# An inverse DFT stage contracted 64 partitions at a time, without the transfers that rearranged its input

## The chip, the core and the metric

One NeuronCore of a Trainium2 chip runs the whole program in one launch. The metric is the device time of one execution in microseconds (us). TensorE (PE) multiplies; its weight loads have a row of their own (PEld). VectorE (DVE) and ScalarE (ACT) work on tiles and read the accumulators; GpSimd (POOL) and SyncE (SP) here only issue DMAs.

## The reference

`x` has 4 batches of 3072 x 256. A frequency mix comes first, then two feed-forward layers. Only the mix is touched by the change.

```python
X = np.fft.rfft(x, axis=1)
Yr = Xr @ w_r - Xi @ w_i + b_r
Yi = Xr @ w_i + Xi @ w_r + b_i
Yr = np.sign(Yr) * np.maximum(np.abs(Yr) - lam, 0.0)      # lam = 0.01, Yi likewise
y = np.fft.irfft(Yr + 1j * Yi, n=3072, axis=1)
# then: k = relu(xk @ w_k); v = (k*k) @ w_v; r = sigmoid(xr @ w_r); x = r * v
# then: h = x @ w_in; out = (h * clip(h + 3, 0, 6) / 6) @ w_out
```

## The kernel before

The transform of 3072 points is split into 96 x 32. `s1` does the 96-point part of a batch `b` in eight steps and stores it to DRAM. `mid(b)` loads it back in 12 chunks `j` (`NP = 12`); each chunk has two frequency groups of 64 rows. `ib` does the last 96-point part of the inverse. What follows (`u_r`, `u_k`, `u_v`) is the first feed-forward layer, in units of 12 matmuls over 512 columns, and then the second layer.

Inside `mid(b)`, chunk `j` goes through:

- `s2(j)`: the 32-point transform, 8 PE instructions, whose output `X` is split by ACT and DVE into a high and a low part (`Xh`, `Xl`).
- `mix(j)`: 18 matmuls over 256 columns, then two kinds of DVE adds into `y` (`yf`), a ReLU on ACT into `m` (`ym`), and one DVE pass (L379) that ends the soft threshold. `y` is laid out [128 partitions, 2, 256]: the partitions hold the two groups, 64 each, and the middle index the real and the imaginary part.
- L380 to L382: four DMAs on SP move quadrants of `y` into `z` (`yz`), so that each group's real and imaginary rows together fill 128 partitions.
- `split_y(j)` (batches 1 to 3 only): ACT and DVE split `z` into `yh` and `yl`.
- `ia(j)`: the 32-point inverse. In batches 1 to 3 these are three matmuls for each of two groups (high x high, low x high, high x low; the type is a rounded 32-bit float), in batch 0 one full 32-bit matmul for each group, which is two PE instructions. All contract 128 partitions. ACT copies the accumulator to `iasb` (L403) and SP stores it.

The order is written out by hand: step `j` of `mid` does `s2(j)`, then, after a yield, `split_y(j - 2)` and `mix(j - 1)`, then, after another yield, `ia(j - behind)`; `behind` is `BEHIND[b]`, 3 for batch 0 and 2 for the others. The last DVE pass of chunk `j` and its four DMAs are issued at the beginning of step `j + 2`. The `mid` of batches 1 to 3 and `s1`, `ib` are interleaved with the feed-forward layer: between two yields of `mid` one or two units of 12 matmuls run. In batch 0 nothing else but weight decoding on ACT and DVE runs beside it. The tables `tt` (three buffers) are loaded by POOL; a tile holds the forward table of one chunk and the inverse table of the chunk `behind` it. The last `ia` of a batch are called from the next part through `ends`.

Each engine takes its instructions in program order, so an ACT instruction that waits holds all ACT instructions behind it.

Of the kernel before, what the change touches and what calls it, by code (L numbers as in the profile page):

```python
# [23 lines left out]
TOK = 512  # L24
NT = S // TOK
LAM = 0.01
BEHIND = (3, 2, 2, 2)
AHEAD = 7

CHUNKS = (1, 2, 3, 4, 5, 6, 7, 0)  # L30
# [19 lines left out]
def _tables():  # L50

    th = 2 * np.pi / S
    n1 = np.arange(N1)
    n2 = np.arange(N2)
    f1 = np.zeros((N1, N1))
    f1[:, 0] = 1.0
    f1[:, 1] = (-1.0) ** n1
    for u in range(1, 48):
        f1[:, 2 * u] = np.cos(2 * np.pi * u * n1 / N1)
        f1[:, 2 * u + 1] = -np.sin(2 * np.pi * u * n1 / N1)  # L60
    fwd = np.zeros((NG, 2, 2, N2, 4, 2, N2))
    inv = np.zeros((NG, 2, 2, N2, 2, 2, N2))
    for g in range(NG):
        for uu in range(2):
            u = 2 * g + uu
            m = np.zeros((2, N2, 2, N2))
            w = np.zeros((2, N2, 2, N2))
            if u:
                k = u + N1 * np.arange(N2)
                s = np.where(k <= S // 2, 1.0, -1.0)  # L70
                c, z = np.cos(th * np.outer(n2, k)), np.sin(th * np.outer(n2, k))
                m[0, :, 0], m[1, :, 0] = c, z
                m[0, :, 1], m[1, :, 1] = -z * s, c * s
                w[0, :, 0], w[1, :, 0] = c.T * 2 / S, (-z * s).T * 2 / S
                w[0, :, 1], w[1, :, 1] = z.T * 2 / S, (c * s).T * 2 / S
            else:
                for j in range(N2):
                    src = 0 if j < 16 else 1
                    f = N1 * j if j < 16 else N1 // 2 + N1 * (j - 16)
                    c, z = np.cos(th * f * n2), np.sin(th * f * n2)  # L80
                    if j == 0:
                        alt = (-1.0) ** n2
                        m[0, :, 0, 0], m[0, :, 1, 0] = 1.0, alt
                        w[0, 0, 0], w[1, 0, 0] = 1.0 / S, alt / S
                    else:
                        m[src, :, 0, j], m[src, :, 1, j] = c, -z
                        w[0, j, src], w[1, j, src] = c * 2 / S, -z * 2 / S
            m = np.concatenate([m, m.sum(2, keepdims=True), 0 * m[:, :, :1]], 2)
            if u == 0:
                m[0, :, 2, 0], m[0, :, 3, 0] = 1.0, alt - 1.0  # L90
                m[:, :, 0:2, 0] = 0.0
            fwd[g, uu, :, :, :, uu] = m
            inv[g, :, uu, :, uu] = w
    fwd = fwd.reshape(NP, 2, 128, 256).transpose(0, 2, 1, 3)
    inv = inv.reshape(NP, 2, 128, 128).transpose(0, 2, 1, 3)
    ext = fwd[0, :, 0, 128:256].astype(np.float32)
    tab = np.zeros((NP + BEHIND[1], 128, 2, 448), np.float32)
    tab[:NP, :, :, 0:192] = fwd[:, :, :, 0:192]
    tab[BEHIND[1] :, :, :, 192:448] = np.concatenate(_pair(inv), 3)
    tab0 = np.zeros((NP + BEHIND[0], 128, 2, 320), np.float32)  # L100
    tab0[:NP, :, :, 0:192] = fwd[:, :, :, 0:192]
    tab0[BEHIND[0] :, :, :, 192:320] = inv
    small = np.concatenate([f1, f1.T], 1).astype(np.float32)
    return [np.ascontiguousarray(a) for a in (tab, tab0, ext, small)]

# [2 lines left out]
def fourier_mix_ffn_kernel(  # L108
# [45 lines left out]
    def ptile(name):  # L154
        return ps.tile([128, 1024], F32, tag="h", name=name)
# [87 lines left out]
    with tc.manual_schedule(engines=order):  # L243
# [68 lines left out]

        def load_t(b, j):

            k = BEHIND[b]
            if j >= NP + k:
                b, j = b + 1, j - NP - k
            if b < B:
                if pad_t:
                    pad(fp, pad_t.pop())  # L320
                t = fp.tile([128, 2, 448], F32R if b else F32, tag="t", bufs=3, name="tt")
                c = slice(0 if j < NP else 192, 192 if j < BEHIND[b] else 448 if b else 320)
                eng = nc.gpsimd if b or j > 2 else nc.scalar
                eng.dma_start(out=t[:, :, c], in_=(tab if b else tab0)[j, :, :, c])
                tt[b, j] = t

        def mid(b):
            gb = sc_b[b].rearrange("(j g c) n d -> j (c n) g d", g=2, c=4)
            xx, yy = {}, {}
            behind = BEHIND[b]  # L330

            def s2(j):
                (a,) = take(1)
# [15 lines left out]
            def mix(j):  # L349
                xh, xl = xx.pop(j)  # L350
                p = ptile("mix")
                k1 = p[:, 512:768]
                part = lambda k, n=128: [
                    ((xh[:, dt, 128 * k : 128 * k + n], xl[:, dt, 128 * k : 128 * k + n]), dt) for dt in range(2)
                ]
                by = lambda w, xs: [(x, (w[0][:, dt], w[1][:, dt])) for x, dt in xs]
                three(k1, by(aw[0], part(2)))
                if pad_y:
                    pad(fp, pad_y.pop())
                y = fp.tile([128, 2, D], F32, tag="y", bufs=2, name="yf")  # L360
                m = fp.tile([128, 2, D], F32, tag="co", bufs=1, name="ym")
                z = fp.tile([128, 2, D], F32, tag="z", bufs=2, name="yz")
                if b:
                    yh = fp.tile([128, 512], F32R, tag="yh", bufs=2, name="yh")
                    yl = fp.tile([128, 512], F32R, tag="yl", bufs=2, name="yl")
                bs = bias[:, 0:2] if j else bias[:, 0::2]
                three(p[:, 0:256], by(aw[2], part(1)))
                pi = by(aw[1], part(0))
                three(p[:, 256:512], pi[:1], last=False)
                if j == 0:  # L370
                    three(p[0:64, 256:512], by(aw[0], part(3, 64)), first=False, last=False)
                three(p[:, 256:512], pi[1:], first=False)
                for a in range(2):
                    nc.vector.tensor_add(y[:, a], k1, bs[:, a])  # L374
                nc.vector.tensor_add(y, y, p[:, 0:512].rearrange("p (a e) -> p a e", a=2))  # L375
                yield
                nc.scalar.activation(m, y, AF.Relu, bias=lam2, scale=-1.0)
                yield
                nc.vector.scalar_tensor_tensor(y, m, -1.0, y, op0=ALU.mult, op1=ALU.max)  # L379
                for g in range(2):  # L380
                    for a in range(2):
                        nc.sync.dma_start(out=z[64 * a : 64 * a + 64, g], in_=y[64 * g : 64 * g + 64, a])  # L382
                z = z.rearrange("p g e -> p (g e)")
                yy[j] = (z, yh, yl) if b else z

            def split_y(j):
                if b:
# [2 lines left out]

            def ia(j):
                y = yy.pop(j)
                t = tt.pop((b, j + behind))[:, :, 192:448]
                p = ptile("ia") if b else pa.tile([128, 512], F32, tag="acc", name="ia0")
                for g in range(2):
                    c = slice(256 * g, 256 * g + 256)
                    if not b:
                        nc.tensor.matmul(p[:, c], t[:, g, 0:128], y[:, c], start=True, stop=True)
                        continue
                    yh, yl = y  # L400
                    three(p[:, c], [((t[:, g, 0:128], t[:, g, 128:256]), (yh[:, c], yl[:, c]))])
                sb = fp.tile([128, 2, D], F32, tag="ia", bufs=2, name="iasb")
                nc.scalar.activation(sb.rearrange("p g d -> p (g d)"), p[:, 0:512], AF.Copy)  # L403
                nc.sync.dma_start(out=gb[j], in_=sb)

            rest = iter(())
            for j in range(NP + 1):
# [2 lines left out]
                    s2(j)  # L410
                if b or j:
                    load_t(b, j + 2)
                if j < NP:
                    yield
                    if j >= 2:
                        split_y(j - 2)
                if j:
                    rest = mix(j - 1)
                    next(rest)
                    fetch(AHEAD if b or j > 6 else 6)  # L420
                    next(rest)
                    yield
                if behind <= j < NP:
                    ia(j - behind)
            next(rest, None)
            split_y(NP - 2)

            def end(j):
                if j == NP - 1:
                    ready.add(("b", b))  # L430
                ia(j)
                if not b and j < NP - 1:
                    load_t(b, j + 6)

            if b:
                ends.extend([lambda: end(NP - 2), lambda: (load_t(b, NP + 3), split_y(NP - 1)), lambda: end(NP - 1)])
            else:
                ends.extend([lambda: end(NP - 3), lambda: end(NP - 2), lambda: end(NP - 1)])

        ysb = {}  # L440

# [435 lines left out]
        def stream(parts):  # L877

            for kind, part in parts:
                if kind == "ib":  # L880
                    if ends:
                        while ends:
                            ends.pop(0)()
                            yield
                        for _ in range(3):
# [223 lines left out]
```

## Time and profile before

| what | value |
|---|---|
| median of three runs | 2034.64 us (2031.91 to 2035.55) |
| the profiled execution | 2030.07 us |
| its span, first to last instruction | 2028.3 us |
| PE busy | 1949.9 us, 96% of the span |
| DVE, ACT busy | 1424.9 us (70%), 1240.8 us (61%) |
| granted TensorE clock, mean | 0.976 |

The profile is of one execution. A granted clock of 1.00 is 2.4 GHz and 0.50 is 1.2 GHz. A matmul's record is longer than its turn on the engine, because matmuls overlap; the time between two starts is what one costs. A wait names the engine that waits, the line, what it waits for, the total, how often, and the longest.

### The profile page before, as it was taken

What the parts mean: (1) busy time and instruction counts of PE and PEld (TensorE: products, weight loads), DVE (VectorE), ACT (ScalarE), POOL (GpSimd) and SP (SyncE); (2) the same over time, 40 slices, a digit from 0 to 9 for tenths busy, and PEclk for the clock granted to TensorE, in tenths of its full rate; (3) what the DMA queues carried; (4) which work ended last, traced back from release to release, by engine and by line L of the source; (5) the groups of instructions that cost most, each with busy time, mean ns of one, the idle gap of its engine ahead of it and who ended that gap; (6) DMA issues with size and microseconds to landing.
All of it is one profiled execution on the core that took longest, in us unless ns stands there. A gap on an engine that the chain in (4) does not pass through costs nothing.

```text
span 2028.3 us, 32930 instructions
## 1 busy us (share of the span) xinstructions
PE 1949.9 (96%) x13352; PEld 1776.3 (88%) x13352; DVE 1424.9 (70%) x1813; ACT 1240.8 (61%) x1766; POOL 35.5 (2%) x61
## 2 busy tenths in 40 slices
PE   6889989998999999999999999999999999999998
PEld 3758777887688778888889999999999999999998
DVE  1756664565456655777768788877887788788876
ACT  2455545454544545777756677667776777677765
POOL 0100000000000000000000000000000000000000
PEclk7979999998999899999999999999999999999999
DMA  8786446544663343222110011001100011001100
GB/s 251 213 255 193 124 119 208 178 136 113 196 189 107 103 140 122 78 86 87 64 42 22 22 32 32 22 22 29 30 28 22 24 31 32 22 23 32 32 11 22
DMA packets 121161, 177.18 MB, mean 87 GB/s; under 512 B 16129, under 2 KB 78209, under 8 KB 121009
## 3 DMA queue, kind: packets, MB, share of 16 engines
q1 hardware_dynamic: 110016, 152.91, 25.0%
q0 software_dynamic: 8768, 20.95, 3.9%
q8 instruction: 105, 1.72, 0.4%
q10 hardware_dynamic: 2224, 1.22, 0.3%
q14 instruction: 48, 0.39, 0.1%
HBM read 99.13 MB, written 63.31 MB: 80 GB/s over the span
## 4 chain that ended last, share of the span: by engine, by line
PE 77%; DVE 8%; DMA 6%; ACT 4%; SPq 3%; issue 1%; ACTq 0%; DVEq 0%
PE oacc L857 25%; PE rq L857 15%; PE acc L168 10%; PE pk L168 9%; PE cc L857 6%; DMA yz<-yf 5%; PE ib L453 3%; PE pr L168 3%; SPq L382 3%; PE s L297 2%; PE s L340 1%; PE mix L168 1%; DVE yf L374 1%; PE pi L168 1%; DVE yf L375 1%
## 5 line engine op out<-in xcount | busy, mean ns | idle before, releaser
L857 PE MATMUL oacc<-wo_hi,gl 128*128 128x256 f32 x1536 | 424.8, 277 | 1.1 <-DVE gl L798 1.1
L857 PE MATMUL oacc<-wo_hi,gh 128*128 128x256 f32 x1536 | 425.0, 277 | 0.0
L857 PE MATMUL oacc<-wo_lo,gh 128*128 128x256 f32 x1536 | 424.3, 276 | 0.0
L857 PEld LDWEIGHTS oacc<-wo_hi,gl 128*128 128x128 f32 x1536 | 288.7, 188 | 1.7 <-DVE gl L798 1.5
L857 PEld LDWEIGHTS oacc<-wo_hi,gh 128*128 128x128 f32 x1536 | 288.2, 188 | 0.2
L857 PEld LDWEIGHTS oacc<-wo_lo,gh 128*128 128x128 f32 x1536 | 288.4, 188 | 0.0
L789 DVE SCALAR_TENSOR_TENSOR g<-g,c 128x1024 f32<-128x1024 f32 x184 | 225.6, 1226 | 51.9 <-ACT g L785 48.1
L798 DVE TENSOR_TENSOR gl<-g,gh 128x1024 fp32r<-128x1024 f32 x184 | 225.3, 1225 | 39.9 <-ACT gh L795 39.9
L785 ACT ACTIVATE g<-c,half 128x1024 f32<-128x1024 f32 x184 | 212.3, 1154 | 5.2 <-DVE c L780 5.1
L857 PE MATMUL rq<-th,sw 128*128 128x256 f32 x1104 | 206.1, 276 | 0.1
L775 ACT ACTIVATE s<-rq 128x256 f32<-128x256 f32 x184 | 70.5, 383 | 208.1 <-PE rq L857 208.1
L795 ACT ACTIVATE gh<-g 128x1024 fp32r<-128x1024 f32 x184 | 193.7, 1053 | 1.9 <-DVE g L789 1.9
L779 DVE TENSOR_TENSOR c<-rq,s 128x512 f32<-128x512 f32 x184 | 126.8, 689 | 88.6 <-ACT s L775 88.5
L857 PEld LDWEIGHTS rq<-th,sw 128*128 128x128 f32 x1104 | 166.2, 188 | 0.4 <-ACT s L764 0.3
L168 PE MATMUL acc<-gh,wv_hi 128*128 128x512 f32 x384 | 159.8, 416 | 0.0
L168 PE MATMUL pk<-kh,wk_hi 128*128 128x512 f32 x384 | 155.7, 405 | 0.1
L857 PE MATMUL rq<-tl,sw 128*128 128x256 f32 x552 | 152.5, 276 | 0.7 <-DVE tl L733 0.7
L596 DVE TENSOR_TENSOR g<-g 128x1024 f32<-128x1024 f32 x76 | 93.0, 1223 | 83.8 <-ACT gh L592 83.4
L168 PE MATMUL acc<-gh,wv_lo 128*128 128x512 f32 x384 | 151.8, 395 | 0.0
L168 PE MATMUL acc<-gl,wv_hi 128*128 128x512 f32 x384 | 151.5, 395 | 0.0
L168 PE MATMUL pk<-kh,wk_lo 128*128 128x512 f32 x384 | 150.5, 392 | 0.0
L168 PE MATMUL pk<-kl,wk_hi 128*128 128x512 f32 x384 | 150.3, 391 | 0.0
(152 smaller groups left out, 4393.4 us busy)
## 6 DMA issues: line engine op xcount, KB each, us to landing
yt<-sc_y SPq DMA_DIRECT2D x23, 608.0 KB, 4.3
tt<-in_tab_dram POOLq DMA_DIRECT2D x30, 448.0 KB, 4.2
a<-in_x_dram SPq DMA_DIRECT2D x64, 192.0 KB, 3.6
sc_a<-s1sb SPq DMA_DIRECT2D x32, 384.0 KB, 4.0
a<-sc_a SPq DMA_DIRECT2D x48, 256.0 KB, 3.7
yz<-yf SPq DMA_DIRECT2D x192, 64.0 KB, 2.5
sc_b<-iasb SPq DMA_DIRECT2D x48, 256.0 KB, 3.2
a<-sc_b SPq DMA_DIRECT2D x64, 192.0 KB, 3.3
```

Of the source, the lines that this page charges most:

```text
L168: nc.tensor.matmul(o, a, c, start=first and i == 0, stop=last and i == n - 1, **kw)
L297: nc.tensor.matmul(p[:N1, 512 * i : 512 * i + 512], f1, flat(a), start=True, stop=True)
L382: nc.sync.dma_start(out=z[64 * a : 64 * a + 64, g], in_=y[64 * g : 64 * g + 64, a])
L453: nc.tensor.matmul(p[:, q, et, i], lhs, fi, start=True, stop=True)
L596: nc.vector.tensor_mul(g, g, g)
L775: nc.scalar.activation(s[:, 3], q, AF.Copy)
L779: nc.vector.tensor_add(c[:, 1::2], two(rq), s[:, 0:2])
L785: nc.scalar.activation(g, c, AF.Relu, bias=half, scale=1.0 / 6.0)
L789: nc.vector.scalar_tensor_tensor(g, g, 1.0, tmp["c"], op0=ALU.min, op1=ALU.mult)
L795: nc.scalar.activation(h, tmp["g"], AF.Copy)
L798: nc.vector.tensor_sub(hg[i, j][1], tmp["g"], hg[i, j][0].bitcast(F32))
L857: return lambda: nc.tensor.matmul(o, lhs, rhs, start=start, stop=stop, skip_group_check=True)
```

## The change

The four DMAs and the tile `z` go. `ia` reads `y` as it is: each group's 64 partitions are contracted by themselves, the real part and then the imaginary part accumulating into the same output, with the two groups' matmuls in turn (`g` is the inner loop). An `ia` of batches 1 to 3 has 12 matmuls of 64 partitions in place of 6 of 128, one of batch 0 four in place of two. Each group writes a PSUM bank of its own; in batch 0 these are the two buffers of `acc`, and ACT copies them with two instructions. The inverse tables are laid out to match. `split_y` splits `y` and is called before the first yield of the step. Batch 0 runs `ia` two chunks behind as the others do. `ends` has two entries.

```diff
-    inv = inv.reshape(NP, 2, 128, 128).transpose(0, 2, 1, 3)
+    inv = inv.reshape(NP, 2, 2, 64, 128).transpose(0, 1, 3, 2, 4).reshape(NP, 128, 2, 128)
...
-                m = fp.tile([128, 2, D], F32, tag="co", bufs=1, name="ym")
-                z = fp.tile([128, 2, D], F32, tag="z", bufs=2, name="yz")
+                m = fp.tile([128, 2, D], F32, tag="co", bufs=2, name="ym")
...
-                for g in range(2):
-                    for a in range(2):
-                        nc.sync.dma_start(out=z[64 * a : 64 * a + 64, g], in_=y[64 * g : 64 * g + 64, a])
-                z = z.rearrange("p g e -> p (g e)")
-                yy[j] = (z, yh, yl) if b else z
+                y = y.rearrange("p a e -> p (a e)")
+                yy[j] = (y, yh, yl) if b else y
...
-                t = tt.pop((b, j + behind))[:, :, 192:448]
-                p = ptile("ia") if b else pa.tile([128, 512], F32, tag="acc", name="ia0")
-                for g in range(2):
-                    c = slice(256 * g, 256 * g + 256)
-                    if not b:
-                        nc.tensor.matmul(p[:, c], t[:, g, 0:128], y[:, c], start=True, stop=True)
-                        continue
-                    yh, yl = y
-                    three(p[:, c], [((t[:, g, 0:128], t[:, g, 128:256]), (yh[:, c], yl[:, c]))])
+                t = tt.pop((b, j + 2))[:, :, 192:448]
+                ys, ts = ((y[0], y[0], y[1]), (0, 128, 0)) if b else ((y,), (0,))
+                if b:
+                    p = ptile("ia").rearrange("p (g f) -> p g f", g=2)[:, :, 0:D]
+                    o = [p[:, g] for g in range(2)]
+                else:
+                    o = [pa.tile([128, 512], F32, tag="acc", name="ia0")[:, 0:D] for _ in range(2)]
+                n = len(ts)
+                for k in range(2 * n):
+                    a, k = k // n, k % n
+                    for g in range(2):
+                        h = slice(64 * g, 64 * g + 64)
+                        nc.tensor.matmul(
+                            o[g],
+                            t[h, a, ts[k] : ts[k] + 128],
+                            ys[k][h, D * a : D * a + D],
+                            start=a + k == 0,
+                            stop=a == 1 and k + 1 == n,
+                        )
                 sb = fp.tile([128, 2, D], F32, tag="ia", bufs=2, name="iasb")
-                nc.scalar.activation(sb.rearrange("p g d -> p (g d)"), p[:, 0:512], AF.Copy)
+                if b:
+                    nc.scalar.activation(sb, p, AF.Copy)
+                else:
+                    for g in range(2):
+                        nc.scalar.activation(sb[:, g], o[g], AF.Copy)
...
+                if j >= 2:
+                    split_y(j - 2)
                 if j < NP:
                     yield
-                    if j >= 2:
-                        split_y(j - 2)
...
-                if behind <= j < NP:
-                    ia(j - behind)
+                if 2 <= j < NP:
+                    ia(j - 2)
...
             def end(j):
-                if j == NP - 1:
+                if j + 1 < NP:
+                    split_y(j + 1)
+                else:
+                    load_t(b, NP + 3)
                     ready.add(("b", b))
                 ia(j)
...
+            ends.extend([lambda: end(NP - 2), lambda: end(NP - 1)])
```

## Rows read from the trace of the kernel before

**Rows 1.** Busy time by stretch: `mid` of batches 0 to 3, then the rest

```profile
core 0: us, PE busy (x) PEld busy (x) DVE busy (x) ACT busy (x) POOL busy (x), PEclk, DMA share, GB/s
37.70:120.00 82.30, 69.30 (x387) 59.18 (x388) 57.51 (x101) 38.87 (x59) 12.66 (x18) 0.90 0.82 241
...
188.00:320.00 132.00, 119.87 (x628) 101.75 (x628) 82.60 (x110) 65.89 (x87) 7.14 (x12) 0.95 0.47 132
...
376.00:522.00 146.00, 134.42 (x712) 115.94 (x712) 90.66 (x120) 68.38 (x90) 7.65 (x13) 0.94 0.45 127
...
590.00:740.00 150.00, 136.89 (x733) 119.11 (x732) 91.35 (x121) 71.15 (x95) 6.22 (x11) 0.95 0.37 105
740.00:2028.00 1288.00, 1281.52 (x9921) 1225.85 (x9919) 1006.60 (x1234) 886.34 (x1296) 0.00 (x0) 1.00 0.14 42
```

**Rows 2.** Waits of PE: for what, total us, times, longest us

```profile
PE ia L168 <- ACT yh L159: 26.0, 13, 4.2
PE ia L398 <- DMA yz<-yf: 12.3, 9, 2.8
...
PE ia L168 <- DVE yl L160: 7.0, 12, 2.7
```

**Rows 3.** Waits of ACT: the largest that names the four DMAs

```profile
ACT yh L159 <- DMA yz<-yf: 84.2, 31, 5.0
```

**Rows 4.** Timeline of one step of batch 1: start us, us, instruction [idle before <-releaser]

```profile
211.18 0.68 DVE L379 SCALAR_TENSOR_TENSOR yf<-ym,yf 128x512 f32<-128x512 f32 x1
...
211.78 0.95 DVE L160 TENSOR_TENSOR Xl<-s,Xh 128x768 fp32r<-128x768 f32 x1
211.89 2.38 SPq L382 DMA_DIRECT2D yz<-yf  x4
...
213.28 0.39 PE L168 MATMUL pk<-kl,wk_hi 128*128 128x512 f32 x1
...
216.50 0.63 ACT L159 ACTIVATE yh<-yz 128x512 fp32r<-128x512 f32 x1 [3.19 <-DMA yz<-yf]
...
217.18 0.65 PE L168 MATMUL ia<-yh,tt 128*128 128x256 f32 x2 [3.51 <-ACT yh L159]
```

**Rows 5.** PE and its granted clock in and after that wait, by stretch

```profile
214.00:216.00 2.00, 0.00 (x0) 1.00 0.78 277
...
222.00:224.00 2.00, 2.00 (x6) 0.50 0.79 237
```

**Rows 6.** Timeline of PE: an undisturbed `ia` of batch 1 and what follows

```profile
192.90 0.40 PE L168 MATMUL ia<-yh,tt 128*128 128x256 f32 x2
...
193.60 0.65 PE L340 MATMUL s<-tt,a 128*128 128x192 f32 x3
```

**Rows 7.** Timeline of PE: an undisturbed `ia` of batch 0 and what follows

```profile
88.88 1.02 PE L398 MATMUL ia<-yz,tt 128*128 128x256 f32 x4
89.74 1.46 PE L340 MATMUL s<-tt,a 128*128 128x192 f32 x8
```

**Rows 8.** Timeline of PE: `mix(0)` enters and leaves a 64-column form

```profile
45.03 0.28 PE L168 MATMUL mix<-aw_lo,Xh 128*128 128x256 f32 x1
45.15 0.28 PE L168 MATMUL mix<-aw_hi,Xh 128*64 128x256 f32 x1
...
45.86 0.28 PE L168 MATMUL mix<-aw_hi,Xh 128*128 128x256 f32 x1
```

**Rows 9.** Groups of weight loads, by form: 128 and 64 columns wide

```profile
L168 PEld LDWEIGHTS mix<-aw_lo,Xh 128*128 128x128 f32 x288 | 55.1, 191 | 0.0
...
L168 PEld LDWEIGHTS mix<-aw_lo,Xh 128*64 128x64 f32 x8 | 1.1, 135 | 0.0
```

**Rows 10.** Timeline of PE: 16 short matmuls of `ib` with a weight load each

```profile
343.13 1.92 PE L453 MATMUL ib<-fi,a 96*128 96x96 f32 x16
344.83 0.47 PE L168 MATMUL pk<-kh,wk_hi 128*128 128x512 f32 x1
```

**Rows 11.** The four DMAs on SP: ns of one issue, min/median/max

```profile
L382 SPq DMA_DIRECT2D yz<-yf x192: 461/587/1492, 49.4 to 727.6; - x192
```

More of the change, by code (lines that the diff above doesn't have):

```diff
@@ L26 @@
 LAM = 0.01
-BEHIND = (3, 2, 2, 2)
 AHEAD = 7
@@ L94, in _tables @@
     fwd = fwd.reshape(NP, 2, 128, 256).transpose(0, 2, 1, 3)
-    inv = inv.reshape(NP, 2, 128, 128).transpose(0, 2, 1, 3)
+    inv = inv.reshape(NP, 2, 2, 64, 128).transpose(0, 1, 3, 2, 4).reshape(NP, 128, 2, 128)
     ext = fwd[0, :, 0, 128:256].astype(np.float32)
[L97 to L102, printed above, removed]
+    fwd = fwd[:, :, :, 0:192]
+    tab = np.zeros((NP + 2, 128, 2, 448), np.float32)
+    tab[:NP, :, :, 0:192] = fwd
+    tab[2:, :, :, 192:448] = np.concatenate(_pair(inv), 3)
+    tab0 = np.zeros((NP + 2, 128, 2, 320), np.float32)
+    tab0[:NP, :, :, 0:192] = fwd
+    tab0[2:, :, :, 192:320] = inv
     small = np.concatenate([f1, f1.T], 1).astype(np.float32)
@@ L313, in load_t @@
         def load_t(b, j):
-            k = BEHIND[b]
-            if j >= NP + k:
-                b, j = b + 1, j - NP - k
+            if j >= NP + 2:
+                b, j = b + 1, j - NP - 2
             if b < B:
@@ L321, in load_t @@
                 t = fp.tile([128, 2, 448], F32R if b else F32, tag="t", bufs=3, name="tt")
-                c = slice(0 if j < NP else 192, 192 if j < BEHIND[b] else 448 if b else 320)
+                c = slice(0 if j < NP else 192, 192 if j < 2 else 448 if b else 320)
                 eng = nc.gpsimd if b or j > 2 else nc.scalar
@@ L329, in mid @@
             xx, yy = {}, {}
-            behind = BEHIND[b]
             def s2(j):
@@ L422, in mid @@
                     yield
-                if behind <= j < NP:
-                    ia(j - behind)
+                if 2 <= j < NP:
+                    ia(j - 2)
             next(rest, None)
-            split_y(NP - 2)
             def end(j):
-                if j == NP - 1:
+                if j + 1 < NP:
+                    split_y(j + 1)
+                else:
+                    load_t(b, NP + 3)
                     ready.add(("b", b))
                 ia(j)
[L432 to L438, printed above, removed]
+            ends.extend([lambda: end(NP - 2), lambda: end(NP - 1)])
         ysb = {}
@@ L881, in stream @@
                     if ends:
-                        while ends:
+                        for _ in range(2):
                             ends.pop(0)()
```

## Prediction

> **What bounds the kernel now.** I read the busy time by stretch first. After 740 us, PE is busy 1281.5 of 1288 us at clock 1.00 [rows 1]: two thirds of the program is a dense stream of matmuls, so a microsecond that PE saves or loses earlier moves the end by about one. What is to be had lies in the four stretches of `mid`. PE is idle there 82.3 - 69.3 = 13.0 us in batch 0 and 12.1, 11.6 and 13.1 us, together 36.8 us, in batches 1 to 3, and the clock is 0.90, 0.95, 0.94 and 0.95 [rows 1].
>
> The list of PE's waits says who ends that idle time: `ia` waits 26.0 us for `yh`, 7.0 us for `yl` and, in batch 0, 12.3 us for the DMAs into `yz` [rows 2]. `yh` in turn is late because ACT waits for the same DMAs, 84.2 us over 31 times [rows 3]. One step shows the order. The DVE pass that completes `y` ends at 211.86; SP issues four DMAs until 214.27; the data lets ACT start `yh` at 216.50; PE has run out of other work at about 213.5 and starts `ia` at 217.18, after 3.51 us of idling [rows 4].
>
> The clock adds to it. During that gap the clock still reads 1.00, and at 222 to 224, with PE busy throughout, it is 0.50, half of 2.4 GHz [rows 5]. Lost time is the stretch times one minus its clock: 0.05 x 132 + 0.06 x 146 + 0.05 x 150 = 22.9 us in batches 1 to 3 and 0.10 x 82.3 = 8.2 us in batch 0 [rows 1]. Some slow time falls on idling, where it costs nothing, so I count 20 us for the former. In batch 0 some lies at the start of the stretch, before any `ia`; I count 5.
>
> **The change, part by part.**
>
> *The DMAs go.* 192 issues at 0.587 us are 113 us of SP's queue [rows 11], and 192 x 64 KB = 12.6 MB of traffic. PE waits for no load inside the three later `mid`, so SP's freed time is worth nothing by itself; in batch 0, where the DMA share is 0.82 [rows 1], it can only help, and I leave that gain out. What counts is the chain: issue and landing, 216.50 - 211.86 = 4.6 us a chunk, leave the path from `y` to `yh`.
>
> *`split_y` comes earlier and reads `y`.* Its instructions and sizes stay. It now stands in ACT's queue behind `Xh` of the same step and waits for DVE's last pass over `y`. In the step shown ACT could begin `yh` at 211.86, ending at 212.49; DVE has `Xl` ahead, until 212.73, and would end `yl`, a pass of the shape of the one at 211.18, at 213.4. PE needs it at 213.5 [rows 4]. So a wait of 3.51 us becomes none, narrowly there. The new wait of ACT for DVE holds what is queued behind it on ACT, the feed-forward unit's copies and squares, by up to 2 us; PE uses a unit's result two units later, which covers that. Without this cover PE would idle about as long, 1 to 2 us a chunk. ACT and DVE are busy 50% and 62% of batch 1's stretch [rows 1], so there is room. I take back 32 of the 36.8 us idle, leaving the last chunks of each batch where `y`, split and `ia` follow closely, and 18 of the 20 us clock: 50 us. The bounds are 0 (every wait replaced by one on DVE) and 57.
>
> *Batch 0, `ia` two chunks behind.* Here `ia` reads `y` directly. What is late next is DVE: it is busy 57.5 of 82.3 us [rows 1], and if the stretch shrinks by 11 us, 81%. It stands between `mix` and `ia` with two kinds of adds and the last pass, with weight decoding between them. So of 12.3 us waiting and 5 us of clock I take 11; bounds 0 and 17. The second ACT copy costs at most the 0.63 us of a full-width ACT pass [rows 4], 12 times, on an ACT that is busy 38.9 of 82.3 us [rows 1]: nothing. The next `ia` now needs both `acc` buffers copied, but comes a whole step later: nothing. POOL's table loads keep their order relative to `ia`: nothing. One `ends` step fewer moves no work: nothing. The extra buffer of `m` and the layout of the tables cost nothing.
>
> *`ia` itself*, the term in dispute. Undisturbed, six matmuls take 193.60 - 192.90 = 0.70 us, 0.117 each [rows 6]; batch 0's four instructions take 0.86 us [rows 7]. Afterwards there are 12 of the same 256 columns, or eight in batch 0. If the two halves run side by side, a pair costs what one did: +0. If they run in turn, +0.70 us x 36 = 25 us, and +0.86 x 12 = 10 us. A middle value comes from the weight loads. A load of 64 columns is 191 - 135 = 56 ns shorter than one of 128 [rows 9], so 128 columns take some 0.11 us; and 16 short matmuls of `ib` with a load each take 1.70 us, 0.106 each, however few columns they stream [rows 10]. If only the matmuls overlap but the loads queue, an `ia` takes 12 x 0.106 = 1.27 us, +0.57 x 36 = 21 us, and batch 0's eight loads, 0.85 us, add nothing. No row of before shows 64 partitions. The matmuls alternate halves and write separate banks, so nothing in their operands makes a pair wait; I take side by side, with 0.1 us per `ia` for the unpaired beginning and end: 5 us.
>
> Entering and leaving the 64-partition form: the 64-column form in `mix(0)` is entered at 0.12 us after the matmul before, its six matmuls take 0.71 us, and it is left without a gap [rows 8]; I take 0.
>
> The Trainium skill, "TensorEngine Tiling (Array Packing)", section Key Properties, says that tiles can load weights and multiply in parallel, which is the first case, but also that a change of the tiling mode drains TensorE. The trace's column form [rows 8] shows no drain; by that rule the time would be that of the third rival below.
>
> *Sum.* 50 + 11 - 5 = 56 us less. The profiled execution took 2030.07 us, its span 2028.3; that makes 1974. The median of the runs stands 4.6 us above the profiled one; I add 4: **1978 us**.
>
> **The rivals.**
>
> 1. *The halves run in turn*, or only their loads do, or the 64-partition form uses the array as if it were one. For it: PE shows one cadence for everything, and a load is as long as a matmul of 256 columns [rows 6, 9]. Against: the operands do not collide. Compared with the forecast, +16 (21 less the 5 allowed) to +30 us: 1994 to 2008, about 2002, as part of batch 0's extra lies under DVE.
> 2. *The wait moves to DVE or ACT.* For it: `yl` is already what `ia` waits for last in 12 cases [rows 2], and in the step shown the split would be ready 0.1 us before its need [rows 4]. Against: their busy shares. If half of 61 us returns, +30: 2008.
> 3. *A drain at every entry and exit.* A 256-column matmul's record of 0.28 us is 0.16 longer than its 0.12 us turn [rows 8]; 2 x 48 x 0.16 = 15 us: 1993. Against: the 64-column form.
> 4. *Slower: each change of half waits until the array is empty.* Then every matmul of an `ia` takes 0.16 + 0.12 = 0.28 us, 3.3 us an `ia`, +2.6 x 36 = 94 us, and batch 0 adds 8 x 0.16 + 0.86 = 2.1 us, 26 in all: 1978 - 5 + 120 = 2093. For it: nothing but that no row excludes it. It decides from 61 / 48 = 1.3 us extra per `ia`.
>
> **How the numbers follow.** The forecast has a chance of 0.44, rival 1 0.30, rival 2 0.10, rival 3 0.08, rival 4 0.05; 0.03 is left for several costs that just cancel the gain. About 0.2%, 4 us, is what a measurement of this kernel tells from no change. Faster has the forecast and rivals 1 to 3, less 0.02 for their worst ends: 0.90; same 0.03; slower 0.07. The lower end takes the upper bounds of the gains: 57 + 17 = 74, 2030 - 74 + 4 = 1960. The upper end, 2010, includes rivals 1 to 3. The likeliest case alone is 1965 to 1990.
>
> **What would show it.** In the profile of the changed kernel: PE's waits for `yh`, `yl` in `ia` below 5 us in sum and none for a DMA in batch 0; the clock of the three later stretches at 0.99 or more; an undisturbed `ia` of batches 1 to 3 near 0.8 us from its first start to the next matmul's (1.3 to 1.4 is rival 1, with 64-row forms whose starts are 0.11 apart; 3 is rival 4); a gap only at its edges is rival 3; ACT or DVE as new releasers of PE is rival 2. The prediction is wrong if the two halves don't overlap, or if DVE in `mid` is late by more than a unit of the feed-forward layer covers.

## The result, and the profile after

The changed kernel takes 1982.47 us in the median (1979.89 to 1986.19, four runs), 0.9746 of the kernel before, with an interval of 0.9726 to 0.9766. The forecast was 1978. Its profiled execution took 1981.2 us with a span of 1979.4; the span is 48.9 us shorter than that of before.

First the busy time by stretch of the changed kernel, with the columns of [rows 1]: `mid` of batches 0 to 3, the rest, and then one long stretch from the first matmul of `pk` (those with `w_k`) to the first of the second layer. That stretch holds batches 1 to 3 and all that is interleaved with them, so the same work lies in it in every kernel here.

```profile
core 0: us, PE busy (x) PEld busy (x) DVE busy (x) ACT busy (x) POOL busy (x), PEclk, DMA share, GB/s
36.80:108.00 71.20, 64.95 (x430) 55.21 (x431) 54.65 (x96) 36.94 (x68) 11.93 (x17) 0.98 0.69 219
...
171.00:300.00 129.00, 126.61 (x739) 104.93 (x739) 84.86 (x114) 70.50 (x94) 7.14 (x12) 0.99 0.42 124
...
358.00:495.00 137.00, 132.18 (x783) 111.21 (x782) 89.83 (x120) 70.31 (x94) 7.67 (x13) 0.99 0.42 122
...
560.00:685.00 125.00, 121.45 (x742) 103.85 (x741) 82.98 (x114) 64.80 (x88) 5.68 (x10) 0.99 0.30 87
685.00:1979.00 1294.00, 1287.66 (x9949) 1230.83 (x9947) 1009.77 (x1238) 888.69 (x1298) 0.00 (x0) 1.00 0.14 42
136.50:980.10 843.60, 832.84 (x4468) 695.19 (x4468) 548.54 (x698) 488.33 (x614) 22.65 (x39) 0.99 0.41 126
```

The same long stretch of the kernel before:

```profile
149.10:1028.80 879.70, 842.88 (x4254) 708.68 (x4253) 549.19 (x697) 488.52 (x613) 22.65 (x39) 0.97 0.44 131
```

Three differences make up the whole: the front, with batch 0, ends at 136.5 instead of 149.1 (12.6 us); the long stretch is 843.6 instead of 879.7 (36.1 us); what follows is equal to 0.2 us (1979.4 - 980.1 = 999.3 against 2028.3 - 1028.8 = 999.5). PE idles 2.4, 4.8 and 3.6 us in batches 1 to 3, 10.8 together, where it was 36.8 [rows 1], and 6.3 us in batch 0, where it was 13.0. The clock of the three stretches is 0.99 instead of 0.95, 0.94 and 0.95.

PE's waits in the changed kernel (those that answer to [rows 2], and the new ones):

```profile
PE s L338 <- issue: 6.6, 3, 2.9
...
PE ia L399 <- ACT iasb L411: 3.2, 4, 1.1
PE mix L168 <- DVE yf L372: 1.9, 1, 1.9
PE ia L399 <- ACT yh L159: 1.5, 1, 1.5
PE ia L399 <- DVE yf L376: 1.5, 3, 0.5
```

The 26.0 us for `yh` are 1.5 now and the 12.3 us for transfers are gone. (Most of the wait put down to `iasb` is DVE's; see batch 0 below.) What ACT waits for before `yh` has changed its name and shrunk from the 84.2 us of [rows 3]:

```profile
ACT yh L159 <- DVE yf L376: 33.6, 16, 3.2
```

The new entry at the top of PE's list, `s2` with "issue" (the profile shows no releaser), can be read from the timeline of such a step in batch 2, by the order of the program and the times:

```profile
374.26 0.68 DVE L376 SCALAR_TENSOR_TENSOR yf<-ym,yf 128x512 f32<-128x512 f32 x1
...
374.98 0.64 ACT L159 ACTIVATE yh<-yf 128x512 fp32r<-128x512 f32 x1 [2.87 <-DVE yf L376]
...
376.46 1.04 ACT L597 ACTIVATE gh<-g 128x1024 fp32r<-128x1024 f32 x1
...
377.54 1.23 DVE L601 TENSOR_TENSOR g<-g 128x1024 f32<-128x1024 f32 x1 [1.13 <-ACT gh L597]
378.80 1.23 DVE L602 TENSOR_TENSOR gl<-g,gh 128x1024 fp32r<-128x1024 f32 x1
379.94 0.75 DVE L371 TENSOR_TENSOR yf<-mix,bias 128x256 f32<-128x256 f32 x2
380.72 0.69 DVE L372 TENSOR_TENSOR yf<-yf,mix 128x512 f32<-128x512 f32 x1
...
381.51 2.90 PE L338 MATMUL s<-tt,a 128*128 128x192 f32 x8 [2.94 <-issue]
```

ACT stands 2.87 us at `yh`, because DVE's last pass over `y` isn't done. Behind `yh` in ACT's queue are `kh` and `gh` of the feed-forward unit, so DVE, which needs `gh`, is held 1.13 us, and DVE's adds of `mix`, queued behind, end at 381.41. They free the accumulators, and `s2` starts 0.1 us later. So the hold explains at most 1.13 of the 2.94 us; the rest is work that stands ahead of the adds in DVE's queue. One such chain a batch, of 1.8 to 2.9 us, makes up 6.6 of the 10.8 us that PE still idles; 1.9 us for DVE's adds and 1.5 us for `yh` are most of the rest.

An undisturbed `ia` of batch 1 and what follows, PE with one weight load (compare [rows 6]):

```profile
180.16 0.39 PE L168 MATMUL acc<-gl,wv_hi 128*128 128x512 f32 x1
...
180.47 0.30 PEld L399 LDWEIGHTS ia<-yh,tt 64*128 64x128 f32 x4 [0.35 <-issue]
180.48 0.50 PE L399 MATMUL ia<-yh,tt 64*128 64x256 f32 x4
180.82 0.28 PE L399 MATMUL ia<-yl,tt 64*128 64x256 f32 x2
180.93 0.39 PE L399 MATMUL ia<-yh,tt 64*128 64x256 f32 x4
181.16 0.28 PE L399 MATMUL ia<-yl,tt 64*128 64x256 f32 x2
181.37 1.57 PE L338 MATMUL s<-tt,a 128*128 128x192 f32 x8
182.64 0.53 PE L168 MATMUL pk<-kh,wk_hi 128*128 128x512 f32 x1
```

The matmuls ahead of the `ia` of [rows 6] and behind its `s2`, in the kernel before:

```profile
192.67 0.39 PE L168 MATMUL acc<-gl,wv_hi 128*128 128x512 f32 x1
...
194.77 0.53 PE L168 MATMUL pk<-kh,wk_hi 128*128 128x512 f32 x1
```

Twelve matmuls take 181.37 - 180.48 = 0.89 us where six took 0.70. Inside, a pair starts every 0.115 us, as one matmul did: the halves run side by side. The rest is at the edges. The weight load of the first matmul isn't pulled ahead of the matmuls before it (idle 0.35 us), and `ia` begins 0.32 us after the matmul before it, where it was 0.23; the next matmul comes late; and the `s2` after it takes 182.64 - 181.37 = 1.27 us, where it took 1.17. Lead, `ia` and `s2` together are 2.48 us instead of 2.10, +0.38 us for an `ia` like this one. Not every one is: of the 36 in this trace, 31 begin 0.32 us after the matmul ahead, 30 take 0.89 to 0.90 us, and 24 are followed by an `s2` of 1.27 us.

### The profile page after: what moved, and what is told of

Same layout as the page of the kernel before. It is cut to its first block, busy times and chain, and to the rows that moved or that the text cites. A ratio compares the mean times of both kernels' runs of the same rounds, so it can differ in the third digit from the quotient of the medians.

```text
span 1979.4 us, 33066 instructions
## 1 busy us (share of the span) xinstructions
PE 1936.1 (98%) x13616; PEld 1758.7 (89%) x13616; DVE 1423.2 (72%) x1813; ACT 1240.0 (63%) x1778; POOL 34.8 (2%) x60
## 4 chain that ended last, share of the span: by engine, by line
PE 91%; DVE 4%; ACT 3%; DMA 1%; issue 1%; ACTq 0%; SPq 0%; DVEq 0%
PE oacc L862 25%; PE rq L862 15%; PE acc L168 13%; PE pk L168 13%; PE cc L862 6%; PE mix L168 4%; PE pr L168 3%; PE ib L458 3%; PE s L338 3%; PE s L297 2%; PE ia L399 2%; PE pi L168 1%; DVE yf L371 1%; DVE yf L372 1%; DVE g L794 0%
## 5 line engine op out<-in xcount | busy, mean ns | idle before, releaser
L593 ACT ACTIVATE g<-pk 128x1024 f32<-128x1024 f32 x96 | 97.7, 1018 | 83.3 <-PE pk L168 82.9
```

The costliest lines, as they stand in the source:

```text
L593: nc.scalar.activation(g, p, AF.Relu)
```

## The experiments

The table has all runs. Ratios are to the kernel before, run on the same chip. The other columns are of one profiled execution, in us: "front" is the start of the first `pk`; "stretch" is the long stretch above; "PE idle" is what of it PE isn't busy; "clock" is the time lost to a granted clock below 1.00 in it, summed over slices of 4 us; "at full clock" is PE's busy time in it less that loss. The loss also counts slow time in which PE idles, so the last column comes out too low where waits are many: counted only while PE is busy, the loss is some 21 us in the kernel before and 27 us in `before_split_early`, which makes 822 and 825 us at full clock. A comparison to 1 or 2 us between executions of the same code can't be made: "front" alone ranges from 136.5 to 140.9 for code that is the same up to there, but for a buffer (changed, `split_late`, `halves_lag3`, `m_one_buffer`, `mixed`).

| run | ratio (95%) | front | stretch | PE idle | clock | at full clock |
|---|---|---|---|---|---|---|
| before | | 149.1 | 879.7 | 36.8 | 22.2 | 820.7 |
| changed | 0.9746 (0.9726 to 0.9766) | 136.5 | 843.6 | 10.8 | 5.1 | 827.7 |
| split_late | 0.9731 (0.9715 to 0.9746) | 138.1 | 837.0 | 7.8 | 0 | 829.2 |
| one_group_then_other | 0.9791 (0.9776 to 0.9805) | 138.5 | 850.8 | 7.5 | 3.4 | 839.9 |
| all_rows | 0.9779 (0.9763 to 0.9796) | 138.5 | 848.5 | 6.8 | 1.7 | 840.0 |
| dead_transfers | 0.9786 (0.9771 to 0.9801) | 146.1 | 842.1 | 11.0 | 3.4 | 827.7 |
| before_lag3 | 0.9721 (0.9689 to 0.9753) | 145.2 | 829.1 | 10.3 | 1.7 | 817.1 |
| before_split_early | 1.0259 (1.0229 to 1.0290) | 148.9 | 938.5 | 86.1 | 41.0 | 811.4 |
| batch0_as_before | 0.9778 (0.9742 to 0.9813) | 147.1 | 844.0 | 11.0 | 5.1 | 827.9 |
| mixed | 0.9695 (0.9677 to 0.9712) | 140.9 | 831.6 | 9.9 | 5.1 | 816.6 |
| halves_lag3 | 0.9708 (0.9692 to 0.9724) | 137.3 | 834.6 | 5.9 | 0 | 828.7 |
| m_one_buffer | 0.9752 (0.9736 to 0.9769) | 139.5 | 843.9 | 11.0 | 5.1 | 827.8 |
| dead_on_pool | 0.9769 (0.9752 to 0.9785) | 140.9 | 845.2 | 11.0 | 6.8 | 827.4 |

### split_late: the split where it stood

The changed kernel with `split_y` after the first yield of the step, as before.

```diff
-                if j >= 2:
-                    split_y(j - 2)
                 if j < NP:
                     yield
+                if j >= 2:
+                    split_y(j - 2)
```

> The changed kernel with split_y(j - 2) back behind the first yield of a step; the transfers stay away. Theory (what counted is that the transfers left the path): within 6 us of the changed kernel, 1976 to 1988 us, with PE idle in the mid of batches 1 to 3 no larger than the 11 us of the changed kernel, since mix and a unit still lie between the split and ia. Rival (the earlier split recovered the wait): 2000 us or more, and PE waits for yh again, 15 us or more.

Measured: 0.9731, and PE's "issue" wait before `s2` is no longer among its waits; `ia` waits 2.9 us for `yl` instead. The stretch is 6.6 us shorter, the ratio 0.0015 lower, with intervals that overlap. That is the theory's outcome: the earlier split is no part of the gain. At the three steps with the chain of the timeline above PE now idles 1.1, 2.1 and 1.1 us, on `yl` and on the `ia` ahead of `s2`, where it idled 1.8, 2.9 and 1.8: the earlier split lengthens this idling by 0.7 to 0.8 us, and costs between nothing and some 6 us in all.

### one_group_then_other: the halves not in turn

The changed kernel with the two loops exchanged: all six matmuls of one group, then the six of the other.

```diff
-                for k in range(2 * n):
-                    a, k = k // n, k % n
-                    for g in range(2):
+                for g in range(2):
+                    for k in range(2 * n):
+                        a, k = k // n, k % n
```

> The changed kernel with all matmuls of group 0 first and then those of group 1, so that neighbours use the same half of the rows. Theory (the halves work side by side only because they alternate): an ia of batches 1 to 3 takes 12 x 0.117 = 1.40 us plus 0.19 at its edges in place of 0.89, so +0.7 x 36 = 25 us, and batch 0 up to 10 us more: 2005 to 2018 us. Rival (PE overlaps the halves in whatever order, or each matmul has half the rows to do and is faster for it): 1980 to 1986 us.

Measured: 0.9791 (1989.89 us), between the times of the two theories, and the stretch 7.2 us longer than the changed kernel's. An `ia` takes 1.25 us instead of 0.89, but not the 1.40 of twelve turns of 0.117. PE's timeline of one `ia` shows why:

```profile
192.41 0.39 PE L168 MATMUL pk<-kl,wk_hi 128*128 128x512 f32 x1
192.72 0.50 PE L399 MATMUL ia<-yh,tt 64*128 64x256 f32 x2
193.06 0.28 PE L399 MATMUL ia<-yl,tt 64*128 64x256 f32 x1
193.07 0.51 PE L399 MATMUL ia<-yh,tt 64*128 64x256 f32 x4
193.41 0.28 PE L399 MATMUL ia<-yl,tt 64*128 64x256 f32 x2
193.53 0.40 PE L399 MATMUL ia<-yh,tt 64*128 64x256 f32 x2
193.77 0.27 PE L399 MATMUL ia<-yl,tt 64*128 64x256 f32 x1
193.97 1.57 PE L338 MATMUL s<-tt,a 128*128 128x192 f32 x8
```

In the program each group is `yh`, `yh`, `yl`, `yh`, `yh`, `yl`, so in program order no four `yh` could stand together and no two `yl`. The records fit two sequences, the second shifted by three places against the first: the second half starts while the first still has three matmuls to go. So, by the records, side by side is a property of the halves, and the alternation in the kernel is worth 0.36 us an `ia` on top.

### all_rows: no halves

The changed kernel with the matmuls contracting all 128 partitions. It mixes the two groups, so the output isn't the reference's; everything but the height of the matmuls stays.

```diff
-                            t[h, a, ts[k] : ts[k] + 128],
-                            ys[k][h, D * a : D * a + D],
+                            t[:, a, ts[k] : ts[k] + 128],
+                            ys[k][:, D * a : D * a + D],
```

> The changed kernel's 12 (batch 0: four) matmuls of ia, each contracting all 128 partitions in place of 64, so the two groups are mixed in the output. Theory (two halves run side by side, a full-height matmul cannot): an ia of batches 1 to 3 takes 12 x 0.117 = 1.40 us without gaps at its edges in place of 0.89, +18 us, and batch 0 up to 9 us more: 1998 to 2010 us. Rival (12 matmuls cost the same whatever their height): 1980 to 1986 us.

Measured: 0.9779 (1987.54 us), again between the two. PE's timeline of one `ia`:

```profile
192.36 0.39 PE L168 MATMUL pk<-kl,wk_hi 128*128 128x512 f32 x1
192.58 0.63 PE L399 MATMUL ia<-yh,tt 128*128 128x256 f32 x4
...
194.00 1.46 PE L338 MATMUL s<-tt,a 128*128 128x192 f32 x8
195.16 0.53 PE L168 MATMUL acc<-gh,wv_hi 128*128 128x512 f32 x1
```

Here the lead is 0.22 us, the `ia` 1.42 (12 x 0.118) and `s2` 1.16: no cost at the edges; that cost is therefore the 64-partition form's. The sum of 2.80 us is 0.32 above the changed kernel's; PE's busy time at full clock is 12.3 us higher, 0.34 for each `ia`. Yet the stretch is only 4.9 us longer, since 4.0 us of idling and 3.4 us of slow clock disappear; that the longer `ia` gives DVE time is the likely reason, and not shown. What is saved on PE here is partly waited for.

### before_lag3: the transfers kept, and read a step later

The kernel before with every batch's `ia` three chunks behind and the split of a chunk a step later. The transfers stay.

```diff
-BEHIND = (3, 2, 2, 2)
+BEHIND = (3, 3, 3, 3)
...
-                    if j >= 2:
-                        split_y(j - 2)
+                if j >= 3:
+                    split_y(j - 3)
...
```

> The kernel before with the transfers kept, and split_y and ia three chunks behind in all batches (in batches 1 to 3 the split of a chunk stands a whole step after its transfers). Theory (the wait was the transfers' latency, and distance hides it as well as leaving them out): the waits and slow clock of batches 1 to 3 go, 45 to 50 us, ia stays at 0.70 us, batch 0 stays: 1983 to 1995 us. Rival (the transfers hold SP or ACT wherever their reader stands): above 2010 us, with ACT waiting for yz still 40 us or more.

Measured: 0.9721 (1977.68 us, below the theory's 1983 to 1995), as fast as the changed kernel, though its batch 0 still waits for the transfers. Its stretch:

```profile
145.20:974.30 829.10, 818.81 (x4253) 693.83 (x4252) 548.24 (x698) 485.57 (x614) 25.10 (x42) 1.00 0.46 140
```

That is 14.5 us less than the changed kernel's 843.6. In batches 1 to 3, what cost the time was the distance between a transfer's issue and its use, not the transfer. With the same matmuls as before, PE's time at full clock is 817.1, not 820.7; the 3.6 us (some 5 if the loss is counted only while PE is busy) are put down to the ends of matmuls ahead of a wait, which are busy in the records and otherwise overlap the next matmul. An estimate agrees: PE has 36 waits in this stretch before and 11 here, and 25 x 0.16 us, by which a record is longer than its turn, are 4 us.

### before_split_early: the transfers kept, the split earlier

The kernel before with the split moved ahead of the yield, as the change does.

```diff
+                if j >= 2:
+                    split_y(j - 2)
                 if j < NP:
                     yield
-                    if j >= 2:
-                        split_y(j - 2)
...
-            split_y(NP - 2)
```

> The kernel before with only split_y moved ahead of the first yield, as the change has it; the transfers stay. Theory (the transfers are the wait): ACT waits for them even earlier, more than 84 us in sum, and the time is the same or longer: 2030 to 2080 us. Rival (the earlier split is the gain): 2010 us or less.

Measured: 1.0259 (2088.34 us), slower as the theory said, and by more. ACT's wait grows from 84.2 us [rows 3] to

```profile
ACT yh L159 <- DMA yz<-yf: 162.3, 35, 7.5
```

and the stretch by 59 us. The same lever as in `before_lag3`, pushed the other way: the distance decides, and the earlier split, harmless without the transfers, is costly with them.

### batch0_as_before: the old form in batch 0 alone

The changed kernel; batch 0 has its four transfers, its `ia` three chunks behind and its full-height matmuls again. `m` has one buffer, for space.

```diff
...
+                if not b:
+                    z = fp.tile([128, 2, D], F32, tag="z", bufs=2, name="yz")
+                    for g in range(2):
+                        for a in range(2):
+                            nc.sync.dma_start(out=z[64 * a : 64 * a + 64, g], in_=y[64 * g : 64 * g + 64, a])
+                    yy[j] = z.rearrange("p g e -> p (g e)")
+                    return
...
```

> The changed kernel with batch 0 as before: transfers, three chunks behind, two full matmuls (m has one buffer for space). Theory: batch 0's part of the gain, forecast at 11 us, goes: 1990 to 1997 us. Rival (batch 0 gains nothing because DVE is late instead): 1980 to 1985 us.

Measured: 0.9778 (1990.32 us, as the theory said), the front at 147.1 and the stretch unchanged at 844.0. Batch 0's part of the gain is 10.6 us by the front and 0.0032, 6.5 us, by the ratio; against `m_one_buffer`, which has one buffer of `m` too, 7.6 us and 0.0026, 5.3 us.

### dead_transfers, m_one_buffer, dead_on_pool: what the issue alone costs

`dead_transfers` is the changed kernel with the four DMAs issued into a tile that nobody reads; the tile's space comes from the second buffer of `m`. `m_one_buffer` takes that buffer away and nothing else. `dead_on_pool` is the first with the DMAs issued by POOL.

```diff
-                m = fp.tile([128, 2, D], F32, tag="co", bufs=2, name="ym")
+                m = fp.tile([128, 2, D], F32, tag="co", bufs=1, name="ym")
+                z = fp.tile([128, 2, D], F32, tag="z", bufs=2, name="yz")
...
+                for g in range(2):
+                    for a in range(2):
+                        nc.sync.dma_start(out=z[64 * a : 64 * a + 64, g], in_=y[64 * g : 64 * g + 64, a])
```

> The changed kernel with the four transfers issued as before into a tile that nobody reads (m has one buffer again for space). Theory (their latency on the path cost the time, not their traffic or SP's queue): 1980 to 1988 us. Rival (192 issues of 0.59 us on SP and 12.6 MB beside the loads cost it): 10 us or more above the changed kernel, with PE waiting for loads.

> The changed kernel with one buffer for m, the control for the kernel with transfers that nobody reads. Theory: nothing, within 4 us of the changed kernel and its first unit at 136 to 139 us. Rival (the missing buffer was the 8 us of that kernel): first unit at 144 us or later.

> The kernel with transfers that nobody reads, but issued by POOL in place of SP. Theory A (SP's queue was the cost: loads of x stand behind the transfers): the first unit moves back to 136 to 140 us. Theory B (their traffic is the cost): it stays at 144 us or later. With the table loads behind them on POOL it could also be later for that reason; then PE waits for tables.

Measured: 0.9786, 0.9752 and 0.9769. One buffer of `m` costs nothing that can be seen. Against it, transfers that nobody waits for cost 0.0034, 6.9 us (between the two expectations), and the front shows where: 146.1 against 139.5, while the stretch is no longer. In `dead_transfers` PE waits longer for the loads of `x`, which come after the transfers in SP's queue:

```profile
PE s L297 <- DMA a<-in_x_dram: 8.6, 6, 2.9
```

In `m_one_buffer` and in `dead_on_pool` that wait is 3.8 us. It isn't the whole account of the 6.6 us: the wait for `ib`'s input is 3 us shorter (1.9 against 5.0), and the granted clock from 120 to 150 us is 0.67 against 0.79. Issued by POOL the transfers move the front by 1.4 us, to 140.9, just above theory A's 136 to 140 and within the scatter, and the ratio by 0.0017, with intervals that overlap. So the larger part of the cost goes with SP's queue, and the traffic has at most the rest.

### mixed and halves_lag3: two ways to put the parts together

`mixed` has batch 0 of the changed kernel (no transfers, halves, two chunks behind), with one buffer of `m`, and batches 1 to 3 of `before_lag3`. `halves_lag3` is the changed kernel with `ia` of batches 1 to 3 three chunks behind, the split a step later and a third buffer of `y`. The core of both edits:

```diff
+BEHIND = (2, 3, 3, 3)
...
-                    split_y(j - 2)
+                    split_y(j - 3)
...
```

> Batch 0 as in the changed kernel (rows in halves, no transfers, two behind), batches 1 to 3 as in the kernel before but with split_y and ia three chunks behind. Theory (the two gains are separate): up to the first unit of the feed-forward layer it gains what the changed kernel gains, 11 to 13 us, and after it what the longer lag gained, 50 us: 1966 to 1974 us. Rival (the shorter batch 0 only moves a wait into the next stage): 1977 us or more.

> The changed kernel with split_y behind the yield and ia three chunks behind in batches 1 to 3 (y has three buffers): beside the kernel mixed it differs only in the rows by halves and the missing transfers of batches 1 to 3. Theory (halves cost 0.89 + 0.09 us against 0.70 an ia at equal waits): 0.28 x 36 = 10 us above mixed. Rival (the transfers cost SP and the DMA engines as much as the halves cost PE): within 3 us of mixed.

Measured: 0.9695 (1971.38 us, as expected) and 0.9708; both are faster than the changed kernel, `mixed` by 0.6% against `m_one_buffer` on the same chip (1971.38 against 1983.26 us). The long stretch, first of `mixed`:

```profile
140.90:972.50 831.60, 821.73 (x4252) 696.62 (x4252) 548.39 (x697) 485.13 (x613) 25.10 (x42) 0.99 0.46 139
```

and of `halves_lag3`:

```profile
137.30:971.90 834.60, 828.72 (x4469) 691.32 (x4469) 548.75 (x698) 487.06 (x614) 25.19 (x42) 1.00 0.42 128
```

The halves make PE's time at full clock 12.1 us longer here (828.7 against 816.6), and the theory had nearly all of that as the difference of the two kernels. It is 3.0 us in the stretch (5.5 against `before_lag3`, whose batches 1 to 3 are those of `mixed`) and not to be told from nothing in the ratio: `halves_lag3` idles 4.0 us less and loses 5.1 us less to the clock. On that point the theory behind the expectation fell, and its rival has the number. As in `all_rows`, a costlier `ia` on PE isn't paid in full. Why PE idles less is not shown: beside the longer `ia`, `halves_lag3` has no transfers in batches 1 to 3 and a third buffer of `y`.

## Why the prediction came out as it did

The direction, the mechanism and the range were right, and the time is 4.5 us above the forecast. By terms, the span fell by 48.9 us where the sum had 56.

- **The wait for the transfers** is gone, as predicted. Idling in batches 1 to 3 fell by 26.0 us, and the ends of matmuls ahead of a wait (see `before_lag3`) add 3.6: 29.6 where 32 was taken.
- **The clock** gave back 22.2 - 5.1 = 17.1 us where 18 was taken.
- **`ia` itself, the edges.** The halves run side by side, as taken: a pair starts every 0.115 us. The step that failed is "Entering and leaving the 64-partition form: ... I take 0", with the 0.1 us allowed for an unpaired beginning and end. PE's time at full clock is 827.4 to 829.2 in all kernels with alternating halves and 816.6 to 817.1 with 128 partitions and few waits; 11 to 12 us over 36 `ia`, 0.3 us each. The timeline's 0.38 would be 14 us, but not every `ia` pays each part: 31 x 0.09 (lead), 30 x 0.19 (`ia`) and 24 x 0.10 (`s2`) come to 11. The 64-column form of [rows 8] was a misleading neighbour: it has no such edges. That is the price of the third rival, 2 x 0.16 us for each `ia`, which had a chance of 0.08, and `all_rows` shows that it belongs to the 64-partition form. The first rival's 25 us for halves in turn was well priced too: `all_rows` stands 840.0 - 816.9 = 23.1 above the 128-partition kernels. The halves win back half of it.

The Trainium skill, "TensorEngine Tiling (Array Packing)", section Key Properties, says that a change of the tiling mode drains TensorE; the trace shows a cost for a visit to this form, 0.3 to 0.4 us, but not that it is a drain: the first matmul of `ia` starts at 180.48 us, before the record of the matmul ahead ends at 180.55, and ends are modelled. Whether it is a drain, or only a weight load that isn't pulled ahead, no run here separates.

- **`split_y` earlier.** The step said that ACT's new wait "holds what is queued behind it on ACT", and that a result used two units later covers that. It named the wait and missed one way out: the cover holds for PE's own use of the unit's result, but DVE waits for the same ACT copy, and DVE's adds of `mix` behind it free the accumulators that `s2` needs. This is the second rival in small: PE idles there 1.8 to 2.9 us a batch, and `split_late` takes 0.7 to 0.8 us of each away.
- **Batch 0** gave 12.6 us where 11 less 1.2 for its `ia` was taken. The waiting for transfers went as said, and 6.3 us of idling remain. "What is late next is DVE" held. The list of waits gives 1.5 us to DVE and 3.2 us to ACT's copies of the two `acc` buffers, but three of the four waits put down to ACT are DVE's by their times. The `ia` at 74.16 starts 0.15 us after the end of DVE's last pass, just as the one at 68.72 does, whose wait is put down to DVE; ACT's copies end only as it starts:

```profile
67.89 0.68 DVE L376 SCALAR_TENSOR_TENSOR yf<-ym,yf 128x512 f32<-128x512 f32 x1
...
68.72 1.14 PE L399 MATMUL ia<-yf,tt 64*128 64x256 f32 x8 [0.49 <-DVE yf L376]
...
69.79 1.57 PE L338 MATMUL s<-tt,a 128*128 128x192 f32 x8
...
73.33 0.68 DVE L376 SCALAR_TENSOR_TENSOR yf<-ym,yf 128x512 f32<-128x512 f32 x1
73.52 0.64 ACT L411 ACTIVATE iasb<-ia 128x256 f32<-128x256 f32 x2
...
74.16 1.18 PE L399 MATMUL ia<-yf,tt 64*128 64x256 f32 x8 [0.68 <-ACT iasb L411]
```

  So DVE has 3.6 us and the copies, which the working had put at nothing, 1.1; in `m_one_buffer` the list itself gives 3.5 us to DVE and 2.5 to the copies. An `ia` takes 69.79 - 68.72 = 1.07 us instead of 0.86 [rows 7], twice the 0.1 us taken. Against these stands the gain that the working left out: SP's freed time in batch 0 "can only help, and I leave that gain out". `dead_transfers` shows that it is about half of batch 0's part, 6 to 7 us, the larger part of it from SP's queue.
- **The rest** is as before, to 0.2 us.

In batches 1 to 3 the sum had 50 - 3.6 = 46.4 us and got -26.0 - 17.1 - 3.6 + 10.6 = -36.1. Of the 10.3 us too few, 7.0 are the edges of `ia`. Batch 0 gave 12.6 - 9.8 = 2.8 us more than its terms, so the sum was 7 us too large (56 against 48.9). The median stands 1.3 us above the profiled execution, where 4 were added; that takes 2.7 off, and 4.5 us remain. Errors of both signs partly cancel, so that the time came this close is in part luck.

Open: how the 6 to 7 us of `dead_transfers` divide between SP's issue time and traffic, and why PE idles less where `ia` is longer.

## What to carry to other kernels

A wait on a transfer can be removed by removing the transfer or by reading it a step later; try the second first, for here it costs a few lines and is worth as much. Transfers that nobody waits for are not free where loads are queued behind them on the same issuing engine. And a microsecond added to or saved on the busiest engine need not count fully, even here: twelve more microseconds of PE work made the long stretch 3 to 7 us longer here. A wait that the profile puts down to one engine is worth comparing with the ends of the other candidates, for the one named may only have ended at the same moment.

## What the hardware did that was not expected

- The 64-partition form of a matmul costs at both edges: its first weight load isn't pulled ahead (0.35 us between the loads), the first start is 0.1 us late, and the block after it takes 0.1 us more. A 64-column form showed none of this [rows 8].
- By the records, matmuls on different halves of the rows don't keep program order, so "Each engine takes its instructions in program order" is not the case for PE there. In `one_group_then_other` the second group's first matmul starts at 193.07 us, with three matmuls of the first group, earlier in the program, still to start.

The Trainium skill, "TensorE: Matmul & The Clock Gate", section Part 3: Packing small matmuls — row/col tiling, calls matmuls monotone in program order in start and end. The records of that run don't agree, for the starts of matmuls on different row halves.
